# Folding w3 and w_out at the start, in two passes around the first attention, and the keys' sums inside the second product

## The chip, the cores and the metric

The kernel runs on one core of one Trainium2 chip, as one launch. The metric is the device time of an execution in microseconds (us). Before the change three runs gave a median of 1324.92 us (1324.34 to 1325.64).

## The reference

Three layers follow each other; all numbers are float32 except the weights of the second layer, which arrive as float64.

1. Attention with pooled keys: q, k and v are (8 batches, 8 heads, 576 positions, 64). Keys and values are averaged over groups of 8 positions, so each head has 72 keys. `attn = softmax(q @ k_p.T / 8)`, `out = attn @ v_p`; the heads are put side by side to `x`, 4608 rows of 512.
2. A gated layer without a nonlinearity: `a = x @ w1`, `b = x @ w2` (512 to 1024), `h = (a * b) @ w3` (1024 to 1024), `x2 = h @ w_out` (1024 to 512).
3. A mixture of 8 experts: `logits = x2 @ w_gate + bias`, the row's best expert is taken, `out = p * (relu(x2 @ w1[e]) @ w2[e])`.

Since nothing stands between w3 and w_out, `(a * b) @ w3 @ w_out` is `(a * b) @ W` with `W = w3 @ w_out` (1024 by 512). The kernel computes W once: this is the fold. It also computes `W @ w_gate` (the gate), whose 8 columns ride along with W, so that logits come out of the same matmuls as x2.

## The kernel before, in words

**Number format.** Every large matmul is made of three with operands split into a high and a low part (`mm3`, L116): high·high, high·low, low·high. Each matmul has 512 columns, or 260 in the second product. A float64 weight tile of 128 by 512 (0.52 MB) is turned into such a pair by `conv` (L390): two ScalarE steps on the two halves of each 8-byte number, two VectorE (DVE) steps that put the float32 together in place (L397, L399), a ScalarE copy to the high part (L400) and a subtraction on GpSimd (POOL) for the low part (L122). There are 40 such tiles: 16 of w3, 8 of w_out, 8 each of w1 and w2.

**Stages.** The 4608 rows go in 9 chunks of 512 (4 tiles of 128).

- Prologue: attention of chunk 0 (`Attention(0)`: K keys' sums, S scores and softmax, V1 values' sums, T transposes, V product), with w1 and w2 tiles 0 to 7 staged in the space of Wh and Wl (`stage`).
- `first_chunk` (L614): the first product of chunk 0 (`mm1`, L531; eight m blocks of 24 matmuls, `prep_w12(m + 2)` hooked behind block m) with scores of chunk 1 behind blocks 1, 3, 5 and 6; then `w_fold` (L433), which holds all eight PSUM banks as eight accumulators, converts w_out and w3 of round j = 0 to 7 and runs 24 matmuls a round; copies of W out of PSUM; `w_gate` (L465); the rest of attention 1; and the second product of chunk 0 (`mm_w`, L551; 4 tiles of 48 matmuls).
- Chunk loop: `next_chunk(ch)` (L635) for ch = 1 to 7 runs the first product of ch with attention ch + 1 hooked behind its blocks, S(0) to S(3) behind blocks 0 to 3, V1 behind 4, T behind 5 to 7, and the second product with V behind tiles 0 and 2 and early loads of `v` behind tile 3.
- Then routing's last part and the experts, which the change does not touch.

**What sets the order.** Inside the chunk loop the order of every engine is the order of the program text. Before it, a planner orders each engine's instructions by their place in the program and by when it expects them to be ready. DMAs are issued by SyncE (SP) in one queue, in order; a DMA that waits for a buffer holds those behind it.

**Lines that matter.** `S(i)` (L358) runs K for its tile, the scores (L270), loads `q` of the next tile (L361, one of two buffers), and K for the next tile. K leads to `prep_k(b)` (L176) when a new batch begins: four DVE sums (L183), two scalings into `kblk` (L188), and the load of the next batch's keys into the buffers just read (L173). The scores of an even tile use the one PSUM pair `sc`; in the chunk loop all tiles do. PSUM has four banks `mm`, two `tp` and the pair `sc`. Seven buffers of 4 KB per partition, `st4`, serve transposed tiles (`aT`, five an attention), early `v` and raw weight tiles.

Of the kernel before, what the change touches and what calls it, by code (L numbers as in the profile page):

```python
# [18 lines left out]
POOL = 8  # L19
# [8 lines left out]
T0 = (0, 1, 2, 3, 4)  # L28
ACT_T, MM_T = (0, 1, 2, 4, 5, 6, 7), (1, 2, 3)
CVN = 2  # L30
V_POOL, RAW = 2, 4
EARLY = 2
S1 = (1, 3, 5, 6)
# [59 lines left out]
def _program(outer, tc, nc, I, out):  # L93
# [68 lines left out]
    def load_k(b):  # L162
        if b == 0:
            kr = abp.tile([P, 4, S], F32, name="kr0", tag="abh")
# [38 lines left out]
    def load_v0():  # L203
        v0.append(abp.tile([P, 4, D, POOL], F32, name="vr0", tag="abl"))
# [7 lines left out]
    def early_v(b):  # L212

        if b < B:
# [41 lines left out]
    def softmax_tile(t):  # L256
        load_q(t)
        q = qs[t]
        if t in MM_T:
            sc = [(tp_ps if t == 3 else mm_ps)("scm") for _ in range(2)]  # L260
# [61 lines left out]
    def attn_V(a, z, aT, xh, xl):  # L322
        kn = slice(0, 6 * TK)
        for pr in range(4):
            ps = mm_ps("avps")[:, :z - a]
# [12 lines left out]
    class Attention:  # L338
# [19 lines left out]
        def S(self, i):  # L358
# [3 lines left out]
            if i < 3:  # L362
                self.K(i + 1)
# [10 lines left out]
        def V(self):  # L374
# [5 lines left out]
            attn_V(a, z, self.aT, *self.x)  # L380
# [27 lines left out]
    names = ("w1h", "w1l", "w2h", "w2l")  # L408
    w_stack = ExitStack()
    w12 = pool(w_stack, "w12")  # L410
    wt12 = [{n: w12.tile([P, 4, P], F32R, name=f"{n}{m}") for n in names} for m in range(8)]
    done_w = set()

    def prep_w12(m):
        if m < 8 and m not in done_w:
            done_w.add(m)
            conv(I["w1"][m], flat(wt12[m]["w1h"]), flat(wt12[m]["w1l"]), staged.get((m, "w1")))
            conv(I["w2"][m], flat(wt12[m]["w2h"]), flat(wt12[m]["w2l"]), staged.get((m, "w2")))


    staged = {}

    def stage(srcs):

        for n, tag in enumerate(("Wh", "Wl")):
            t = wp.tile([P, 4, 512], I64, name="stage", tag=tag)
            for i, (k, src) in enumerate(srcs[4 * n:4 * n + 4]):
                nc.sync.dma_start(t[:, i], src)
                staged[k] = t[:, i]

    fold = [((j, k), I["wo"][j] if k == "wo" else I["w3"][j, k]) for j in range(8) for k in ("wo", 0, 1)]

    def w_fold():  # L433
        sc = psum.tile([P, 2, 512], F32, name="wps3", tag="sc", bufs=1)
        accs = [sc[:, 0], sc[:, 1]] + [tp_ps("wps2") for _ in range(2)] + [mm_ps("wps") for _ in range(4)]
        for j in range(8):
            if j == 1:
                for k, src in fold[8:8 + CVN]:
                    staged[k] = load64(src)
                stage(fold[8 + CVN:16 + CVN])  # L440
            wo = st4("wo", (P, 2, 512), F32R)
            conv(I["wo"][j], wo[:, 0], wo[:, 1], staged.get((j, "wo")))
            if j == 0:
                w3 = [st4("w3", (P, 2, 4, P), F32R) for _ in range(2)]
            else:
                w3 = xp.tile([P, 2, 2, 4, P], F32R, name="w3", tag=("xh", "xl")[j % 2])
                w3 = [w3[:, 0], w3[:, 1]]
            for h in range(2):
                conv(I["w3"][j, h], flat(w3[h][:, 0]), flat(w3[h][:, 1]), staged.get((j, h)))
                for k in range(4):  # L450
                    mm3(accs[4 * h + k], w3[h][:, 0, k], w3[h][:, 1, k], wo[:, 0], wo[:, 1], j == 0, j == 7)
        Wh = wp.tile([P, 8, 2, 260], F32R, name="Wh", tag="Wh")
        Wl = wp.tile([P, 8, 2, 260], F32R, name="Wl", tag="Wl")

        wfs = []
        for kb in range(8):
            w2v = accs[kb].rearrange("p (h n) -> p h n", h=2)
            nc.scalar.copy(Wh[:, kb, :, :256], w2v)
            wf = st4("wf", (P, 2, 256), F32)
            (nc.scalar.copy if kb % 2 else nc.vector.tensor_copy)(wf, w2v)  # L460
            nc.vector.tensor_tensor(Wl[:, kb, :, :256], w2v, Wh[:, kb, :, :256].bitcast(F32), op=ALU.subtract)
            wfs.append(wf)
        return Wh, Wl, wfs

    def w_gate(Wh, Wl, wfs):  # L465

        gT = st4("gT", (E, 2, 512), F32)
        for half in range(2):
            wT = xp.tile([P, 4, 4, P], F32, name="wT", tag=("xh", "xl")[half])
            for k in range(4):  # L470
                tps = tp_ps("wtp", (P, 4, P))
                wf = wfs[4 * half + k]
                for nb in range(4):
                    nc.tensor.transpose(tps[:, nb], wf[:, nb // 2, P * (nb % 2):P * (nb % 2) + P], ident)
                (nc.scalar.copy if k % 2 else nc.vector.tensor_copy)(wT[:, :, k], tps)
            g = mm_ps("wgp")
            for nb in range(4):
                nc.tensor.matmul(g[:E], lhsT=wg[:, nb], rhs=flat(wT[:, nb]), start=nb == 0, stop=nb == 3)
            nc.scalar.copy(gT[:, half], g[:E])
        gp = tp_ps("wgt", (P, 8, 2, 4))  # L480
        for kb in range(8):
            nc.tensor.transpose(gp[:, kb].rearrange("p a b -> p (a b)"), gT[:, kb // 4, P * (kb % 4):P * (kb % 4) + P], ident[:E, :E])
        nc.scalar.copy(Wh[:, :, :, 256:260], gp)  # L483
        nc.vector.tensor_tensor(Wl[:, :, :, 256:260], gp, Wh[:, :, :, 256:260].bitcast(F32), op=ALU.subtract)

    att = Attention(0)
    att.K(0)
    for t in range(1, 4):
        load_q(t)
    nc.sync.dma_start(c, I["c"])  # L490
    load_v0()
    stage([((m, k), I[k][m]) for m in range(4) for k in ("w1", "w2")])
    for i in range(4):
        att.S(i)
        if i == 0:
# [432 lines left out]
```

## Time and profile before

| | |
|---|---|
| runs, median (lowest to highest) | 1324.92 us (1324.34 to 1325.64) |
| profiled execution, own time | 1322.37 us |
| its span | 1320.6 us, 17555 instructions |
| PE, matmuls | busy 1236.5 us (94%), 6518 instructions |
| DVE | busy 676.7 us (51%), 1325 |
| ScalarE (ACT) | busy 381.9 us (29%), 813 |
| POOL | busy 405.2 us (31%), 463 |
| TensorE's granted clock, mean | 0.970 of full speed |
| DMA | 126.99 MB, mean 96 GB/s |

The span runs from the first to the last instruction; the execution's own time is 1.8 us longer. Shares are means over stages that differ: DVE has 51% over the whole span and far more in some stretches, so each stage is read by itself. Matmuls are pipelined, so that a matmul's duration is longer than the distance between the starts of two; work is counted by that distance. A wait is read from the idle time in front of an instruction and from what ended it. A granted clock of 1.00 is 2.4 GHz, 0.50 is 1.2 GHz.

### The profile page before, as it was taken

The page shows a single profiled execution, that of the slowest core. Times are in us where ns is not written, and L with a number is a line of the kernel's source. Part 1 is how long each engine was busy: PE and PEld are TensorE (multiplying, and loading weights), DVE is VectorE, ACT ScalarE, POOL GpSimd, SP SyncE. Part 2 cuts the span into 40 slices and gives each one's busy share as a digit, 9 for nine tenths or more (in the row PEclk, how much of TensorE's full clock was granted, in tenths as well). Part 3 has the DMA queues.
Part 4 walks back from the last instruction along what each step waited for, and adds up shares of the span by engine and source line. Part 5 has one row for each costly group of instructions (what it writes and reads, how often), then busy time and mean ns, then how long its engine had stood idle before and what let it go on. Part 6 is the DMA issues. An engine that isn't in the chain of part 4 may idle for free. (4 is left out here: it accounts for less than half of the span.)

```text
span 1320.6 us, 17555 instructions
## 1 busy us (share of the span) xinstructions
PE 1236.5 (94%) x6518; PEld 1048.9 (79%) x6518; DVE 676.7 (51%) x1325; ACT 381.9 (29%) x813; POOL 405.2 (31%) x463
## 2 busy tenths in 40 slices
PE   4988798999989989999899999999999999999987
PEld 3766577897978979879789798887888888888877
DVE  6999525436344363343543523745464474556442
ACT  5786532322322223223222221211222212222211
POOL 3576301402314014050140301314543344244242
PEclk7989898999999999999999999998999999999998
DMA  8545212012021130210202001305441442344140
GB/s 291 211 167 202 91 49 80 9 65 79 17 77 52 47 97 9 93 44 25 84 1 87 14 25 50 127 24 184 176 170 46 176 176 95 121 175 168 53 170 18
DMA packets 53371, 126.99 MB, mean 96 GB/s; under 512 B 12668, under 2 KB 12924, under 8 KB 53244
## 3 DMA queue, kind: packets, MB, share of 16 engines
q1 hardware_dynamic: 45884, 105.89, 23.2%
q0 software_dynamic: 7232, 19.71, 3.8%
q8 instruction: 57, 0.93, 0.3%
q14 instruction: 54, 0.44, 0.1%
q10 hardware_dynamic: 144, 0.02, 0.0%
HBM read 105.62 MB, written 20.55 MB: 96 GB/s over the span
## 5 line engine op out<-in xcount | busy, mean ns | idle before, releaser
L299 POOL TENSOR_TENSOR ex<-ex,sm 128x576 f32<-128x576 f32 x35 | 40.5, 1157 | 442.8 <-DVE sm L293 423.7
L117 PE MATMUL e<-xh,e1h 128*128 128x512 f32 (+2 forms) x320 | 122.4, 383 | 5.7 <-issue 4.5
L118 PE MATMUL e<-xl,e1h 128*128 128x512 f32 (+2 forms) x320 | 123.0, 384 | 0.0
L117 PE MATMUL w<-xh,w1h 128*128 128x512 f32 x288 | 120.2, 417 | 1.9 <-ACT w1h L400 1.9
L119 PE MATMUL e<-xh,e1l 128*128 128x512 f32 (+2 forms) x320 | 121.4, 379 | 0.6 <-issue 0.6
L119 PE MATMUL e<-e2h,abl 128*128 128x512 f32 x296 | 117.8, 398 | 3.5 <-DVE abl L738 3.5
L117 PE MATMUL e<-e2h,abh 128*128 128x512 f32 x296 | 118.3, 400 | 1.3 <-DVE abl L738 1.3
L119 PE MATMUL w<-xh,w1l 128*128 128x512 f32 x288 | 115.7, 402 | 2.8 <-POOL w1l L122 2.8
L561 PE MATMUL x2ps<-Wh,abh 128*128 128x260 f32 x576 | 117.4, 285 | 0.3 <-ACT Wh L483 0.3
L561 PE MATMUL x2ps<-Wl,abh 128*128 128x260 f32 x576 | 116.6, 283 | 0.0
L118 PE MATMUL e<-e2l,abh 128*128 128x512 f32 x296 | 116.4, 393 | 0.0
L561 PE MATMUL x2ps<-Wh,abl 128*128 128x260 f32 x576 | 115.9, 283 | 0.0
L117 PE MATMUL w<-xh,w2h 128*128 128x512 f32 x288 | 113.3, 393 | 2.8 <-DVE asb L545 2.8
L118 PE MATMUL w<-xl,w1h 128*128 128x512 f32 x288 | 115.4, 401 | 0.0
L545 DVE TENSOR_TENSOR asb<-asb,w 128x512 f32<-128x512 f32 x72 | 49.4, 686 | 126.2 <-PE w L119 79.4
L119 PE MATMUL w<-xh,w2l 128*128 128x512 f32 x288 | 113.3, 393 | 0.0
L118 PE MATMUL w<-xl,w2h 128*128 128x512 f32 x288 | 112.8, 392 | 0.0
L546 ACT CAST abh<-asb 128x512 fp32r<-128x512 f32 x72 | 44.6, 620 | 192.3 <-DVE asb L545 192.3
L737 ACT ACTIVATE abh<-e 128x512 fp32r<-128x512 f32 (+2 forms) x80 | 45.4, 567 | 169.8 <-PE e L119 157.2
L750 POOL DMA_INDIRECT out<-o,idc x37 | 37.5, 1012 | 182.7 <-ACT o L749 161.9
L566 DVE TENSOR_TENSOR lg<-x2ps,bias 128x4 f32<-128x4 f32 x72 | 11.6, 162 | 155.9 <-ACT x L565 151.9
L561 PEld LDWEIGHTS x2ps<-Wh,abh 128*128 128x128 f32 x576 | 89.3, 188 | 0.7 <-ACT Wh L483 0.4
(203 smaller groups left out, 2650.6 us busy)
## 6 DMA issues: line engine op xcount, KB each, us to landing
raw<-ew_in SPq DMA_DIRECT2D x80, 512.0 KB
stage<-w_in SPq DMA_DIRECT2D x19, 512.0 KB
kr<-k_in SPq DMA_DIRECT2D x32, 288.0 KB
q<-q_in SPq DMA_DIRECT2D x36, 256.0 KB
vr<-v_in SPq DMA_DIRECT2D x36, 256.0 KB
x2d<-x SPq DMA_DIRECT2D x36, 256.0 KB
cv<-w_in SPq DMA_DIRECT2D x13, 512.0 KB
vr<-v_in SPq DMA_DIRECT2D x54, 64.0 KB
```

Source lines behind the costliest of these rows:

```text
L117: nc.tensor.matmul(ps, lhsT=wh, rhs=xh, start=start, stop=False)
L118: nc.tensor.matmul(ps, lhsT=wh, rhs=xl, start=False, stop=False)
L119: nc.tensor.matmul(ps, lhsT=wl, rhs=xh, start=False, stop=stop)
L299: eng.tensor_tensor(e3, e3, bc(sm.unsqueeze(2), [P, H, SP_]), op=ALU.mult)
L545: nc.vector.tensor_tensor(a, a, ps[1], op=ALU.mult)
L546: nc.scalar.copy(abh[:, m], a)
L561: nc.tensor.matmul(pss[hf][:, :260], lhsT=l[:, m, cols], rhs=r[:, m, hf], start=m == 0 and r is Wh and l is abh, stop=m == 7 and l is abl)
L566: nc.vector.tensor_tensor(lg[:, i, 4 * hf:4 * hf + 4], pss[hf][:, 256:260], bias[:, t, 4 * hf:4 * hf + 4], op=ALU.add)
L737: nc.scalar.activation(hT[0][:, m, :w], ps[:, :w], AF.Relu)
L750: nc.gpsimd.indirect_dma_start(out=out, out_offset=bass.IndirectOffsetOnAxis(idc[:, i, 0:1], 0), in_=o, in_offset=None, bounds_check=N - 1 ...
```

## The change

- The fold comes first, in two passes. Pass one (`accs`, the four `mm` banks) takes the w_out tiles and the first half of w3; rounds 0 to 3 of it follow S(0) to S(3) of attention 0, round 4 V1, rounds 5 and 6 T. Then V. Pass two (`accs2`: `sc` and the two `tp` banks) takes the second half of w3. The converted w3 and w_out tiles lie in the space that w1 and w2 get afterwards; raw tiles go through a ring of eleven buffers (Wh, Wl and free parts of the two 16 KB buffers of k and v), each loaded when the one eleven places before has been converted.
- `conv` writes its intermediate values to a contiguous scratch buffer (`scr`, one of `st4`) in place of the strided halves of the raw tile.
- W's copies out of PSUM follow pass two and the conversion of w1 and w2 tile 0; gate and the rest of attention 1 are hooked into the first product of chunk 0; the values of batch 1 are loaded early there.
- `S(i)` loads `q` two tiles ahead. In the chunk loop the keys' sums and the load of the next keys no longer follow S; they are hooked behind tile 1 of the second product of the chunk before.
- The first attention's V uses the `tp` banks; tile 2's scores use `sc`, tile 1's `tp`.

The diff, cut to its core:

```diff
-ACT_T, MM_T = (0, 1, 2, 4, 5, 6, 7), (1, 2, 3)
+ACT_T, MM_T = (0, 1, 2, 4, 5, 6, 7), (1, 3)
...
-        if b < B:
+        if b < B and b not in v_raw:
             pairs = [st4("vr2", (P, 2, D, POOL), F32) for _ in range(3)]
...
             load_q(4 * self.ch + i + 1)
-            if i < 3:
+            load_q(4 * self.ch + i + 2)
+            if i < 3 and self.ch < 2:
                 self.K(i + 1)
...
-            attn_V(a, z, self.aT, *self.x)
+            attn_V(a, z, self.aT, *self.x, tp_ps if self.ch == 0 else mm_ps)
...
+    def conv(raw, hi, lo):
+        s = st4("scr", (P, 2, 512), I32)
+        f, m, t = s[:, 0].bitcast(F32), s[:, 0], s[:, 1]
+        nc.scalar.activation(f, raw.bitcast(F32)[:, 1::2], AF.Copy, scale=float(2.0 ** -112))
+
+        nc.scalar.activation(t, raw.bitcast(U32)[:, 0::2], AF.Copy, scale=TOP_S, bias=TOP_B)
+        nc.vector.scalar_tensor_tensor(out=t, in0=m, scalar=3, in1=t, op0=ALU.logical_shift_left, op1=ALU.bitwise_or)
+        nc.vector.scalar_tensor_tensor(out=m, in0=m, scalar=-2147483648, in1=t, op0=ALU.bitwise_and, op1=ALU.bitwise_or)
         nc.scalar.copy(hi, f)
         sub_pool(lo, f, hi)
...
+    ring = [x[:, i] for x in [wp.tile([P, 4, 512], I64, name="stage", tag=tag) for tag in ("Wh", "Wl")] for i in range(4)]
+    ring += [ab0["abl"][:, 1024:1536], ab0["abl"][:, 1536:2048], ab0["abh"][:, 1152:1664]]
...
+    wf = [w12.tile([P, 2, 2, 512], F32R, name=f"f{m}", tag=w_tag(m), bufs=1) for m in range(8)]
+    w3s = [wf[j // 2][:, j % 2] for j in range(8)]
+    wos = [wf[4 + j // 2][:, j % 2] for j in range(8)]
+    order = [x for j in range(8) for x in (("wo", j), ("w3", j, 0))] + [("w3", j, 1) for j in range(8)]
...
+    def fold_conv(k):
+        dst = wos[k[1]] if k[0] == "wo" else w3s[k[1]]
+        conv(raws[k], dst[:, 0], dst[:, 1])
+        fold_load()
+
+    def fold_mm(accs, j):
+        w3, wo = w3s[j].rearrange("p t (k n) -> p t k n", k=4), wos[j]
+        for k in range(4):
+            mm3(accs[k], w3[:, 0, k], w3[:, 1, k], wo[:, 0], wo[:, 1], j == 0, j == 7)
...
+    accs = [mm_ps("wps") for _ in range(4)]
+    for j in range(8):
+        if j < 4:
+            att.S(j)
+        if j == 4:
+            att.V1()
+        if j == 5:
+            sct = psum.tile([P, 2, 512], F32, name="sct", tag="sc", bufs=1)
+            att.T((0, 1), {0: sct[:, 0], 1: sct[:, 1]})
+            att.T((2, 3))
+        if j == 6:
+            sct = psum.tile([P, 2, 512], F32, name="sct", tag="sc", bufs=1)
+            att.T((4,), {4: sct[:, 0], 5: sct[:, 1]})
+        for k in order[2 * j:2 * j + 2]:
+            fold_conv(k)
+        fold_mm(accs, j)
+    att.V()
...
+    accs2 = [sc[:, 0], sc[:, 1]] + [tp_ps("wps2") for _ in range(2)]
+    for j in range(8):
+        fold_conv(order[16 + j])
+        fold_mm(accs2, j)
     prep_w12(0)
...
+    wfs = [fold_out(accs, 0)]
+    wfs.append(fold_out(accs2, 1))
+    W = (Wh, Wl)
+    prep_w12(1)
...
         h1 = {m: [lambda m=m: prep_w12(m + 2)] for m in range(8)}
-        for n, m in enumerate(S1):
-            h1[m].append(lambda n=n: att.S(n))
-        h1[0] += [lambda: att.K(0)]
-        h1[3] += [lambda: stage(fold[:8])]
+        h1[0] += [lambda: att.K(0), lambda: w_gate_out(w_gate(wfs[0]), 0)]
+        h1[1] += [lambda: w_gate_out(w_gate(wfs[1]), 1)]
+        for i in range(4):
+            h1[i + 1] += [lambda i=i: att.S(i)]
+        h1[4] += [lambda: early_v(1)]
+        h1[6] += [att.V1, lambda: att.T((0, 1))]
+        h1[7] += [lambda: load_k(2), lambda: att.T((2, 3)), lambda: att.T((4,))]
         ab = mm1(0, x_first, h1)
-        W = w_fold()
-        w_gate(*W)
...
-        mm_w(0, ab, lgs[0], {0: [att.V], 2: [att.V], 3: [lambda: early_v(2)]}, W)
+        mm_w(0, ab, lgs[0], {0: [att.V], 1: [lambda: need(prep_k, 2)], 2: [att.V], 3: [lambda: early_v(2)]}, W)
...
-        mm_w(ch, ab, lgs[ch % 2], {0: [att.V], 2: [att.V], 3: [lambda: early_v(b)]}, W)
+        mm_w(ch, ab, lgs[ch % 2], {0: [att.V], 1: [lambda: need(prep_k, b)], 2: [att.V], 3: [lambda: early_v(b)]}, W)
```

`fold_out` copies four accumulators out of PSUM with the three instructions that `w_fold` had for each (L458, L460, L461); `w_gate` now takes one half of W, with two half-size copies where one whole copy stood (L475), and `w_gate_out` writes the gate's columns of that half.

## Rows read from the trace of the kernel before

**Rows 1.** Busy time by stage: length, PE, PEld, DVE, ACT, POOL, clock, DMA share, GB/s.

```profile
0.00:36.00 36.00, 19.18 (x70) 15.12 (x71) 22.67 (x52) 19.24 (x70) 12.71 (x28) 0.76 0.88 294
36.00:133.00 97.00, 85.94 (x363) 67.46 (x362) 93.06 (x116) 76.00 (x179) 61.61 (x46) 0.95 0.53 191
133.00:175.00 42.00, 34.17 (x131) 19.99 (x130) 19.39 (x29) 20.54 (x37) 10.49 (x7) 0.88 0.22 76
211.25:797.95 586.70, 558.05 (x3313) 494.73 (x3313) 257.68 (x604) 152.27 (x320) 131.06 (x220) 0.98 0.16 50
797.95:1320.60 522.65, 503.06 (x2382) 417.57 (x2381) 273.03 (x492) 104.01 (x182) 189.29 (x164) 0.98 0.33 121
```

**Rows 2.** Timeline around the prologue's end: start, duration, instruction, idle before it.

```profile
147.28 0.69 DVE L399 SCALAR_TENSOR_TENSOR cv<-cv 128x512 int32<-128x512 int32 x1
...
174.94 0.51 PE L561 MATMUL x2ps<-Wh,abh 128*128 128x260 f32 x2 [0.30 <-ACT Wh L483]
```

**Rows 3.** PE's waits, 178 to 760 us: waiter, releaser, sum, times, longest.

```profile
PE sc L270 <- DMA q<-q_in: 18.7, 6, 4.4
PE sc L270 <- issue: 8.4, 3, 4.3
PE sc L270 <- DVE kblk L188: 1.3, 1, 1.3
```

**Rows 4.** Timeline of PE, second scores of two chunks.

```profile
222.24 2.26 PE L270 MATMUL sc<-kblk,q 128*128 128x144 f32 x8 [4.28 <-issue]
...
305.50 3.76 PE L270 MATMUL sc<-kblk,q 128*64 128x144 f32 x16 [2.62 <-DMA q<-q_in]
```

**Rows 5.** Timeline of DVE ahead of 222.24 us.

```profile
216.18 0.76 DVE L289 TENSOR_TENSOR ex<-sc,mx 128x576 f32<-128x576 f32 x1
...
218.80 2.68 DVE L183 TENSOR_REDUCE ks<-kr 128x72 f32<-128x576 f32 x4
221.51 0.62 DVE L188 TENSOR_SCALAR kblk<-ks 64x288 f32<-64x288 f32 x2
```

**Rows 6.** Timeline of SP's queue ahead of 305.50 us.

```profile
293.78 3.95 SPq L199 DMA_DIRECT2D vr<-v_in  x6
297.77 0.42 SPq L254 DMA_DIRECT2D q<-q_in  x1
```

**Rows 7.** Timeline of PE in the fold, at either clock.

```profile
103.15 0.39 PE L119 MATMUL wps<-wo,w 128*128 128x512 f32 x1
103.38 0.39 PE L117 MATMUL wps<-wo,w 128*128 128x512 f32 x1
...
125.80 0.63 PE L118 MATMUL wps<-wo,w 128*128 128x512 f32 x1
126.22 0.63 PE L119 MATMUL wps<-wo,w 128*128 128x512 f32 x1
```

**Rows 8.** Busy time in one second product (columns as in Rows 1).

```profile
269.00:292.00 23.00, 23.00 (x181) 22.77 (x181) 6.52 (x22) 6.76 (x20) 0.00 (x0) 1.00 0.09 35
```

**Rows 9.** Busy time behind two of the waits (columns as in Rows 1).

```profile
222.00:230.00 8.00, 7.76 (x28) 6.68 (x29) 4.16 (x8) 1.89 (x3) 1.62 (x3) 0.68 0.53 166
...
646.00:650.00 4.00, 4.00 (x18) 3.30 (x17) 2.65 (x5) 1.15 (x2) 0.00 (x0) 0.87 0.23 70
```

**Rows 10.** Timeline of DVE, then POOL, in the fold.

```profile
122.16 0.68 DVE L397 SCALAR_TENSOR_TENSOR stage<-stage 128x512 int32<-128x512 int32 x1
...
126.45 1.80 DVE L399 SCALAR_TENSOR_TENSOR stage<-stage 128x512 int32<-128x512 int32 x1
...
126.40 1.30 POOL L122 TENSOR_TENSOR wo<-stage,wo 128x512 fp32r<-128x512 f32 x1
```

**Rows 11.** Groups by line, 0 to 178 us: busy, mean ns, idle before.

```profile
L399 DVE SCALAR_TENSOR_TENSOR stage<-stage 128x512 int32<-128x512 int32 x24 | 24.8, 1045 | 0.3
L397 DVE SCALAR_TENSOR_TENSOR stage<-stage 128x512 int32<-128x512 int32 x24 | 22.5, 944 | 1.5 <-ACT stage L396 1.4
...
L299 POOL TENSOR_TENSOR ex<-ex,sm 128x576 f32<-128x576 f32 x7 | 8.4, 1198 | 10.7 <-DVE sm L293 6.1 <-ACT vbt L246 3.9 <-ACT wo L400 0.7
```

More of the change, by code (lines that the diff above doesn't have):

```diff
@@ L163, in load_k @@
         if b == 0:
-            kr = abp.tile([P, 4, S], F32, name="kr0", tag="abh")
+            kr = ab0["abh"].bitcast(F32)[:, :4 * S].rearrange("p (a s) -> p a s", a=4)
             for pr in range(4):
@@ L203, in load_v0 @@
     def load_v0():
-        v0.append(abp.tile([P, 4, D, POOL], F32, name="vr0", tag="abl"))
+        v0.append(ab0["abl"].bitcast(F32)[:, :2048].rearrange("p (a d w) -> p a d w", a=4, d=D))
         v0.append([at.tile([P, D, POOL], F32, name="vr", tag="raw", bufs=RAW) for _ in range(2)])
@@ L259, in softmax_tile @@
         if t in MM_T:
-            sc = [(tp_ps if t == 3 else mm_ps)("scm") for _ in range(2)]
+            sc = [tp_ps("scm") for _ in range(2)]
         else:
@@ L405, in run @@
             f()
-    names = ("w1h", "w1l", "w2h", "w2l")
     w_stack = ExitStack()
     w12 = pool(w_stack, "w12")
-    wt12 = [{n: w12.tile([P, 4, P], F32R, name=f"{n}{m}") for n in names} for m in range(8)]
-    done_w = set()
-    def prep_w12(m):
[L415 to L418, printed above, removed]
@@ L421, in _program @@
[L421 to L463, printed above, removed]
@@ L465, in w_gate @@
[L465 to L484, printed above, removed]
+    ab0 = {n: abp.tile([P, 2048], I64, name=f"early{n}", tag=n) for n in ("abh", "abl")}
@@ new lines, in fold_out, with w_gate @@
+    def fold_out(accs, h):
+        wf = w12.tile([P, 4, 2, 256], F32, name="wf", tag=w_tag(4 + h), bufs=1)
+        for k in range(4):
+            kb = 4 * h + k
+            w2v = accs[k].rearrange("p (h n) -> p h n", h=2)
+            nc.scalar.copy(Wh[:, kb, :, :256], w2v)
+            (nc.scalar.copy if k % 2 else nc.vector.tensor_copy)(wf[:, k], w2v)
+            nc.vector.tensor_tensor(Wl[:, kb, :, :256], w2v, Wh[:, kb, :, :256].bitcast(F32), op=ALU.subtract)
+        return wf
+    def w_gate(wf):
+        wT = [st4("wT", (P, 2, 4, P), F32) for _ in range(2)]
+        for k in range(4):
+            tps = tp_ps("wtp", (P, 4, P))
+            for nb in range(4):
+                nc.tensor.transpose(tps[:, nb], wf[:, k, nb // 2, P * (nb % 2):P * (nb % 2) + P], ident)
+            for n in range(2):
+                (nc.scalar.copy if k % 2 else nc.vector.tensor_copy)(wT[n][:, :, k], tps[:, 2 * n:2 * n + 2])
+        g = tp_ps("wgp")
+        for nb in range(4):
+            nc.tensor.matmul(g[:E], lhsT=wg[:, nb], rhs=flat(wT[nb // 2][:, nb % 2]), start=nb == 0, stop=nb == 3)
+        gT = st2("gT", (E, 512))
+        nc.scalar.copy(gT, g[:E])
+        return gT
@@ new lines, in w_gate_out, with load_w12 @@
+    def w_gate_out(gT, h):
+        gp = tp_ps("wgt", (P, 4, 2, 4))
+        for k in range(4):
+            nc.tensor.transpose(gp[:, k].rearrange("p a b -> p (a b)"), gT[:, P * k:P * k + P], ident[:E, :E])
+        kb = slice(4 * h, 4 * h + 4)
+        nc.scalar.copy(Wh[:, kb, :, 256:260], gp)
+        nc.vector.tensor_tensor(Wl[:, kb, :, 256:260], gp, Wh[:, kb, :, 256:260].bitcast(F32), op=ALU.subtract)
+    names = ("w1h", "w1l", "w2h", "w2l")
+    wt12 = []
+    raw12 = {}
+    def load_w12(m):
+        if m < 8 and m not in raw12:
+            raw12[m] = [load64(I[n][m], st4("cv", (P, 512), I64)) for n in ("w1", "w2")]
@@ L486, in _program @@
+    def prep_w12(m):
+        if m < 8 and m == len(wt12):
+            load_w12(m)
+            t = w12.tile([P, 4, 4, P], F32R, name=f"w{m}", tag=w_tag(m), bufs=1)
+            wt12.append({n: t[:, i] for i, n in enumerate(names)})
+            for i in range(2):
+                conv(raw12[m][i], flat(t[:, 2 * i]), flat(t[:, 2 * i + 1]))
     att = Attention(0)
+    fold_load()
+    fold_load()
     att.K(0)
+    nc.sync.dma_start(c, I["c"])
+    for _ in range(2):
+        fold_load()
     for t in range(1, 4):
@@ L489, in _program @@
         load_q(t)
-    nc.sync.dma_start(c, I["c"])
+    for _ in range(3):
+        fold_load()
     load_v0()
[L492 to L495, printed above, removed]
-            need(prep_v1, 0)
-    att.V1()
-    att.T(T0, [tp_ps("atp") for _ in range(2)] + [mm_ps("atp") for _ in range(4)])
-    prep_w12(0)
-    att.V()
-    for m in range(1, EARLY):
-        prep_w12(m)
-    nc.scalar.dma_start(wg, I["wg"])
+    for _ in range(4):
+        fold_load()
```

49 lines of the change are left out of this document (19 added, 30 removed).

## The prediction

> **What bounds the kernel now.** The page's first part gives TensorE (PE) 94% of the span: at most 84 us are idle, plus what a lower clock costs. I then cut the span into stages [rows 1]. The last one, from 797.95 us on, holds nothing that the diff touches; its 522.65 us stay. Two parts remain.
>
> The prologue ends where the second product of chunk 0 starts, at 174.94 us [rows 2]. VectorE (DVE) is what to read there: busy 22.67 of the first 36 us, 93.06 of the next 97, 19.39 of the last 42 [rows 1]. So it is the bound in the middle (96%) and has 39.9 us free at the two ends: at the start little but the first attention is given to it, and after the last `conv` (147.28 us [rows 2]) fold copies and gate run as a chain between PE, ScalarE and DVE.
>
> In the chunk loop, 211.25 to 797.95 us, that is seven chunks of 83.8 us, DVE is busy 257.68 of 586.70 us and PE 558.05 [rows 1]: PE is the bound, and its losses are in the list of its waits. Three rows hold nearly all: the score matmuls wait 18.7 us for `q` in six places, 8.4 us for "issue" in three, 1.3 us for `kblk` [rows 3], together 28.4 us. The second kind is keys' sums too: PE stands 4.28 us until 222.24 [rows 4], while DVE runs the sums from 218.80 and the scaling to 222.13 [rows 5].
>
> **The change part by part.**
>
> *Chunk loop: q.* The load of `q` is issued at 297.77, behind the `v` tail loads from 293.78 on the same queue (SP) [rows 6], and PE gets it at 305.50 after 2.62 us [rows 4]. The change loads two tiles ahead. The load issued after a chunk's first scores is then for the third tile: it lands at about 305.4 again, and is wanted one m block after 302.9, where PE now arrives at the second scores (305.50 − 2.62). A block is 24 matmuls at 0.227 (103.15 to 103.38 us [rows 7]) and about 1.1 us of scores, 6.6 us, so it is wanted at 309.5: 4 us to spare. A `q` buffer is free once the scores of two tiles before are done; SP waits there for these matmuls, and behind it stand only loads wanted later. All 18.7 us go.
>
> *Chunk loop: keys' sums.* The 2.68 + 0.62 us of DVE work [rows 5] move from between the blocks of the first product to behind tile 1 of the second. There PE is busy 23.00 of 23 us and DVE 6.52 [rows 8], so 3.3 us lie beside matmuls; behind them on DVE wait the logits of tile 2, due a tile (a quarter of the 23 us) later. The load of the next keys, which waits for these sums on SP, moves with them; x2d stores and early `v` loads stand behind it, none wanted within the stage. If that cover went, the cost would be the same 3.3 us a chunk. The 8.4 + 1.3 us go. What is late next is the score bank: DVE frees it at 216.94 [rows 5] and PE would come at 217.96 (222.24 − 4.28), so nothing.
>
> *Chunk loop: clock.* After the longer waits the granted clock is at 1.2 GHz for a while: mean 0.68 over 222 to 230 us, 0.87 over 646 to 650, first and last of six such stretches [rows 9]. Twice (1 − clock) times the length gives the time at the lower level, 18 us over the six, of which half, 9 us, is lost. It goes with the waits. Loop: 28.4 + 9 = 37 us. Bounds: if only the keys' waits go, 9.7 us and a third of the clock's, 13 us; all, 38.
>
> *Prologue: DVE's budget.* The kinds of work do not change: 40 `conv`s (24 for w3 and w_out, 16 for w1 and w2), two attentions, fold copies, gate. DVE was busy 22.67 + 93.06 + 19.39 = 135.1 us before the second product [rows 1]. Added: the last five subtractions behind the second attention's transposes, which now run after 175 us, 5 × 0.68; eight more copies in the gate, of half size, half of them on DVE at about 0.4 (an estimate from 0.68 for the whole size): 5 us, so 140. A private scratch in place of work on the strided halves I count as nothing; a strided DVE step alone takes 0.68 us [rows 10], as long as DVE's other steps of 512, which bounds the gain by a few hundredths of a microsecond a step and the loss likewise. What DVE cannot fill: the first raw tiles (two of 0.52 MB at 294 GB/s [rows 1], and a first latency) arrive at about 5 us, and the last block of the first product, 24 × 0.227 = 5.4 us, follows the last conversion. Between, the saturated stretch idles 4%; I take 8%, 11 us, since in the first pass transfers gate too: the first keys stand behind two raw tiles (3.6 us), and 24 raw tiles with the attention's 4 MB need 56 us of the queue. Sum 5 + 140 + 11 + 5 = 161 us, against 175: a gain of 14. Bounds: no bubbles, 150 (gain 25); all 39.9 us of idle kept and the 5 us added, 180 (loss 5).
>
> *Prologue: PE as a check.* The fold's 192 matmuls (43.6 us) no longer stand behind the first product; half of them lie beside the first attention. Until that product begins, 26 `conv`s pass DVE at 1.99 us each (1.045 + 0.944 [rows 11]), 52 us, with the first attention's 23, the 5 us at the start and 8%: 86 us. All eight PSUM banks are held by the two passes' sums until the fold copies have run, some 4 us more. PE was busy 139.3 us before 175 [rows 1]; without the fold's 43.6 and the first 36 us' 19.2 it then owes at most 76, less at full clock: 155 to 166. 161 stands.
>
> *A rule weighed.* A DVE step of `conv` takes 0.68 us alone and 1.80 where GpSimd's (POOL's) subtraction of 1.30 us began just before it [rows 10]. The Trainium skill, "SBUF — State Buffer", section "Who interferes with whom", says why: a DVE instruction with two SBUF inputs and a GpSimd instruction share a port pair, and whoever issues first holds it for the whole instruction. The trace agrees (1.80 against 0.68). This speaks against packing conversions densely, and is a rival below.
>
> **The sum.** 14 + 37 = 51 us off the profiled execution's 1322.37 gives 1271. That execution lies 2.5 us under the runs' median (1324.92), so I predict 1273 us; own range 1260 to 1285.
>
> **The rivals.**
>
> *DVE and POOL exclude each other, and this sets the prologue.* A `conv` needs 2 × 0.6 on DVE and 1.30 on POOL, one after the other: 2.5 us, 100 for forty. With POOL's 8.4 us of normalising [rows 11], DVE's 55 us of other work (135 − 40 × 1.99) beside none of it and 10 at the ends, 173: no gain. For it: mean steps of 0.944 and 1.045 against 0.68 [rows 10, 11]. Against: if DVE's other work reads PSUM or sums one operand, it can lie beside POOL. Loop alone: 1322.4 − 37 + 2.5 = 1288.
>
> *Low clock in the passes.* In pass one PE has 12 matmuls per two conversions, 2.7 us in some 5. In the first 36 us, with many gaps, the clock was 0.76 in the mean; in the saturated stretch, where the fold also waited between bursts, 0.95 [rows 1]. At 0.43 us a matmul (125.80 to 126.22 [rows 7]) the passes cost 82 us in place of 44; with attention at the same level the first product starts about 18 us later: 1273 + 18 = 1291. The Trainium skill, "TensorE: Matmul & The Clock Gate", section "HAM oscillation — how this bites in real kernels", describes bursts between waits that run cold every time; the 0.95 agrees only in part.
>
> *q still late.* If the loads land late whatever the distance, the loop gives 13: 1322.4 − 14 − 13 + 2.5 = 1298. Against it: the 4 us to spare.
>
> *DVE fully packed.* 150 us in place of 161: 1262.
>
> *Slower: scratch buffers starve the conversions.* Each `conv` now also needs one of the seven buffers called st4, which five transposed tiles, three early `v` pairs, the raw w1 and w2 tiles and the gate's transposes share. With one left, a `conv` is a chain: three ScalarE steps (some 2 us by DVE's 0.68 for the same size), DVE 1.99, POOL 1.30, so 5.3 us, against 3.8 in the forecast (151 us over 40). At 1.5 each the 51 us are used up when 34 of 40 go so; with all, 1333. Against: five tiles are held only from round 5 of pass one to the end of the first attention, which leaves two, and the `v` pairs come when two loads are left.
>
> **How the numbers follow.** Forecast 0.52, exclusion 0.17, low clock 0.08, q late 0.09, fully packed 0.08, slower 0.06. The range 1250 to 1303 holds the first five: under 1260 since DVE's stretched steps may stretch less, above 1298 for two cases together. A difference under 0.2% (2.6 us) can't be told from none here; only a few of the starving cases end there: 0.02. Slower 0.06, faster 0.92.
>
> **What would show it.** In the changed profile: no PE wait of over 1 us for `q` or keys' sums in the loop, chunks of about 78.5 us at a clock of 1.00, the sums inside the second product's stretch; the second product of chunk 0 starting at about 161 us, DVE over 85% busy from 6 us on. Wrong if that start is at 175 or later, if the score matmuls wait for something new (the bank, PSUM), or if `conv`s come more than 4 us apart while DVE idles.

## The result, and the profile after

The changed kernel takes 1278.1 us (median; 1274.7 to 1281.2) beside 1324.6 us of the kernel before on the same chip: ratio 0.9649, 95% interval 0.9617 to 0.9681, 46 us less. The forecast was 1273, its range 1250 to 1303. The total agrees, its two terms do not: the loop gave 42 us where 37 were forecast; the prologue, where 14 were, gave 3 (up to the start of chunk 1 in the profiled executions) to 5 (put in alone, `e3` below).

Busy time by stage of the profiled execution (1275.6 us, span 1273.8), columns as in [rows 1]; the fourth row is the same work as there, from the start of chunk 1 to the end of the seventh loop chunk:

```profile
0.00:36.00 36.00, 18.70 (x63) 13.39 (x64) 24.50 (x45) 21.00 (x70) 18.35 (x29) 0.92 0.92 323
36.00:133.00 97.00, 82.16 (x334) 56.76 (x333) 80.64 (x115) 67.16 (x138) 46.78 (x34) 0.93 0.49 164
133.00:175.00 42.00, 38.10 (x181) 31.31 (x181) 28.15 (x46) 26.83 (x85) 16.21 (x17) 0.96 0.36 118
208.31:753.38 545.07, 544.90 (x3315) 486.24 (x3314) 256.58 (x598) 151.38 (x320) 132.46 (x220) 1.00 0.16 49
753.38:1273.80 520.42, 501.08 (x2382) 416.09 (x2381) 271.50 (x492) 103.99 (x182) 189.15 (x164) 0.99 0.33 122
```

The loop fell from 586.70 to 545.07 us, 41.6 less, 77.9 a chunk. PE is now busy 544.90 of 545.07: nothing is left there but its own matmuls. The last stage, which the diff does not touch, is 2.2 us shorter. PE's waits from 130 to 760 us (waiter, releaser, sum, times, longest) answer to [rows 3]; the prologue's last 44 us are in the window too:

```profile
PE w L113 <- ACT w L394: 1.7, 1, 1.7
PE sc L266 <- ACT ex L281: 1.2, 1, 1.2
PE w L115 <- POOL w L118: 1.1, 1, 1.1
PE rps L624 <- DVE r_oh L617: 0.2, 1, 0.2
```

The waits for `q`, "issue" and `kblk` are gone; the first three of these four lie in the prologue. The keys' sums now run inside the second product, on DVE between the logits of two tiles, as this stretch of DVE's timeline shows (start, duration, instruction, idle before it; it answers to [rows 5, 8]):

```profile
503.09 0.43 DVE L592 TENSOR_TENSOR lg<-x2ps,bias 128x4 f32<-128x4 f32 x2 [3.64 <-ACT x L591]
503.44 2.72 DVE L179 TENSOR_REDUCE ks<-kr 128x72 f32<-128x576 f32 x4
506.20 0.62 DVE L184 TENSOR_SCALAR kblk<-ks 64x288 f32<-64x288 f32 x2
508.90 0.44 DVE L592 TENSOR_TENSOR lg<-x2ps,bias 128x4 f32<-128x4 f32 x2 [2.08 <-ACT x L591]
```

DVE is idle again after them for 2.08 us until the next tile's logits: the cover holds.

The prologue's end answers to [rows 2]. The view lists the operations of one tile name: duration (ns, least/median/most), first to last start. The first row is the first product of chunk 0, the second the second products:

```profile
L113 PE MATMUL w<-xh,w x64: 387/389/628, 98.3 to 172.6; 128*128 128x512 f32 x64
...
L587 PE MATMUL x2ps<-Wh,abh x576: 278/282/393, 174.1 to 821.8; 128*128 128x260 f32 x192
```

The second product begins at 174.1 us in place of 174.94; 161 was forecast. Until 174.1 DVE is busy 132.4 us (24.50 + 80.64 + 28.15, less the last 0.9 us), against 135.1 before: so it idles 42 us where the forecast left it 21. Its conversion steps up to the first product are as long as they were in [rows 11] (line groups, 0 to 98 us: busy, mean ns, idle before):

```profile
L393 DVE SCALAR_TENSOR_TENSOR scr<-scr 128x512 int32<-128x512 int32 x26 | 26.7, 1033 | 0.5
L392 DVE SCALAR_TENSOR_TENSOR scr<-scr 128x512 int32<-128x512 int32 x27 | 24.9, 926 | 1.1 <-ACT scr L391 1.0
```

### The profile page after: what moved, and what is told of

The parts are those of the page before. It is cut to its first block, busy times and chain, and to the rows that moved or that the text cites. A ratio compares the mean times of both kernels' runs of the same rounds, so it can differ in the third digit from the quotient of the medians.

```text
span 1273.8 us, 17569 instructions
## 1 busy us (share of the span) xinstructions
PE 1218.2 (96%) x6518; PEld 1035.8 (81%) x6518; DVE 672.2 (53%) x1329; ACT 379.7 (30%) x818; POOL 403.0 (32%) x463
## 5 line engine op out<-in xcount | busy, mean ns | idle before, releaser
L113 PE MATMUL w<-xh,w 128*128 128x512 f32 x576 | 230.2, 400 | 4.0 <-DVE asb L571 2.3
L115 PE MATMUL w<-xh,w 128*128 128x512 f32 x576 | 226.5, 393 | 1.1 <-POOL w L118 1.1
L114 PE MATMUL w<-xl,w 128*128 128x512 f32 x576 | 225.2, 391 | 0.0
L113 PEld LDWEIGHTS w<-xh,w 128*128 128x128 f32 x576 | 108.8, 189 | 26.8 <-DVE asb L571 2.7
L115 PEld LDWEIGHTS w<-xh,w 128*128 128x128 f32 x576 | 108.8, 189 | 24.7 <-POOL w L118 1.5
L114 PEld LDWEIGHTS w<-xl,w 128*128 128x128 f32 x576 | 108.7, 189 | 21.8 <-issue 0.9
L769 POOL DMA_INDIRECT out<-o,idc x37 | 37.5, 1014 | 183.3 <-ACT o L768 168.8
L587 PEld LDWEIGHTS x2ps<-Wl,abh 128*128 128x128 f32 x576 | 88.9, 188 | 0.0
```

Source lines behind the costliest of these rows:

```text
L113: nc.tensor.matmul(ps, lhsT=wh, rhs=xh, start=start, stop=False)
L114: nc.tensor.matmul(ps, lhsT=wh, rhs=xl, start=False, stop=False)
L115: nc.tensor.matmul(ps, lhsT=wl, rhs=xh, start=False, stop=stop)
L587: nc.tensor.matmul(pss[hf][:, :260], lhsT=l[:, m, cols], rhs=r[:, m, hf], start=m == 0 and r is Wh and l is abh, stop=m == 7 and l is abl)
L769: nc.gpsimd.indirect_dma_start(out=out, out_offset=bass.IndirectOffsetOnAxis(idc[:, i, 0:1], 0), in_=o, in_offset=None, bounds_check=N - 1 ...
```

## Experiments

Chips differ by a few microseconds, so ratios to the kernel before on the same chip are compared; 0.001 is 1.3 us.

**The two halves alone.** Each half of the change was put in without the other.

`e3_prologue_alone` is the changed kernel with both loop edits taken back (and the hook behind tile 1 removed):

```diff
-            load_q(4 * self.ch + i + 2)
-            if i < 3 and self.ch < 2:
+            if i < 3:
```

> The changed kernel with both edits of the loop undone: only the new prologue is left. Theory (the loop is the gain): 1278 and 42 us, about 1320 us, 2 to 5 us under the kernel before. Rival (the prologue gives the 14 us that were forecast, part of it hidden in the loop): about 1310 us.

Measured: 1314.9 us, 0.9959 (0.9938 to 0.9981). The prologue alone is worth 5 us (2.5 to 8): the theory's 2 to 5, not the rival's 10 and more.

`e4_loop_alone` is the kernel before with these edits alone:

> The kernel before with the two edits of the loop alone (q two ahead, keys' sums behind tile 1 of the second product); the fold stays behind the first product. Theory (the loop is the gain): about 1282 us. Rival (loop and prologue need each other, since the early values of batch 1 free the buffers for the keys): over 1295 us.

Measured: 1276.8 us, 0.9688 (0.9657 to 0.9719): 41 us, and no difference from the changed kernel that the intervals can tell. PE's waits from 205 to 760 us have one row left, and the second product starts at 175.8:

```profile
PE rps L599 <- DVE r_oh L592: 0.2, 1, 0.2
...
L562 PE MATMUL x2ps<-Wh,abh x576: 278/282/393, 175.8 to 825.1; 128*128 128x260 f32 x192
```

41 + 5 = 46: the halves add up, and the loop is nearly all of it.

**The loop's two edits, each taken back alone.** `e1_q_one_ahead` drops the second load:

```diff
             load_q(4 * self.ch + i + 1)
-            load_q(4 * self.ch + i + 2)
```

> The changed kernel with q loaded one tile ahead again; all else as changed. Theory (distance): the load behind a chunk's first scores still stands behind ten loads of v, so the second scores of each chunk wait 2.4 to 4.4 us again, about 19 us of waits and some 8 us at the lower clock: about 1304 us. Rival (keys' load in the way): q was late since the next keys' load, which waits for the sums, stood in front of it on the queue; with the sums moved, one tile ahead is enough: about 1279 us.

Measured: 1298.7 us, 0.9843 (0.9822 to 0.9864). PE's waits from 205 to 760 us:

```profile
PE sc L266 <- DMA q<-q_in: 14.1, 5, 4.0
```

So distance is what the second load brings; a `q` one tile ahead is late again. The clock goes with it: for the loop's matmuls PE is busy 553.90 us (208 to 776 us, mean clock 0.98), 9 more than the 544.90 at 1.00 in the changed kernel.

`e2_keys_behind_scores` lets the keys' sums follow the scores as before:

```diff
-            if i < 3 and self.ch < 2:
+            if i < 3:
                 self.K(i + 1)
...
-        mm_w(ch, ab, lgs[ch % 2], {0: [att.V], 1: [lambda: need(prep_k, b)], 2: [att.V], 3: [lambda: early_v(b)]}, W)
+        mm_w(ch, ab, lgs[ch % 2], {0: [att.V], 2: [att.V], 3: [lambda: early_v(b)]}, W)
```

> The changed kernel with the keys' sums behind the scores in the first product again; q stays two ahead. Theory: the waits for keys' sums return, 9.7 us and some 5 us at the lower clock: about 1293 us, with PE waiting in front of the scores only in chunks in which a new batch begins. Rival: with q in time PE comes earlier to the scores and waits longer for the same sums, 3.3 us in each of seven chunks and more clock: about 1305 us.

Measured: 1308.6 us, 0.9922 (0.9892 to 0.9952), the rival's result. The same view:

```profile
PE sc L266 <- issue: 10.4, 3, 4.3
PE sc L266 <- DVE kblk L184: 6.8, 3, 3.1
```

The sums' waits are 17.2 us here; beside late loads they were 9.7 [rows 3]. PE no longer waits for `q`, comes sooner to the same sums, and waits there instead. From the prologue alone (0.9959) the `q` load alone brings 0.0037 (5 us, which the two intervals can hardly tell from nothing), the keys alone 0.0116 (15 us; the lower bound of the prediction was 13 for this case), both 0.031 (41 us).

**What holds the prologue.** `a1_changed_again` repeats the changed kernel beside the next ones:

> The changed kernel itself, on the same chip as the others: 1275 to 1281 us, the second product of chunk 0 at about 174 us.

Measured: 1277.5 us, 0.967 (0.9639 to 0.9701), second product from 175.0. Over the five profiled executions with this prologue (the changed kernel twice, e1, e2 and e3, whose edits are aimed at the loop) that start lies between 173.6 and 176.5 us, so a difference of some 3 us between two single executions tells nothing.

`p1_low_parts_zero` takes the subtraction from POOL: the low parts of all 40 converted tiles are filled with zeros there:

```diff
-        sub_pool(lo, f, hi)
+        nc.gpsimd.memset(lo.bitcast(F32), 0.0)
```

> The changed kernel with the low parts of all 40 converted weight tiles set to zero by a POOL fill in place of the subtraction; everything else runs as before on the same tiles. POOL then reads nothing for a conversion. Exclusion theory (DVE and POOL in turn set the prologue): DVE's two steps fall to 0.68 us each, both passes are through by about 80 us instead of 98, and the second product of chunk 0 starts at about 158 or sooner instead of 174. PE theory (from the end of the passes on, PE's own 68 us of matmuls set the pace): the passes end some 10 us sooner, and the first product still takes about 72 us.

Measured: 1263.4 us in one execution, span 1261.5. Tiles, and DVE's groups from 0 to 174 us:

```profile
L113 PE MATMUL w<-xh,w x64: 389/389/632, 91.7 to 158.8; 128*128 128x512 f32 x64
...
L587 PE MATMUL x2ps<-Wh,abh x576: 277/282/393, 160.2 to 807.8; 128*128 128x260 f32 x192
...
L392 DVE SCALAR_TENSOR_TENSOR scr<-scr 128x512 int32<-128x512 int32 x40 | 28.6, 718 | 7.9 <-ACT scr L391 7.7
L393 DVE SCALAR_TENSOR_TENSOR scr<-scr 128x512 int32<-128x512 int32 x40 | 27.5, 693 | 0.8
```

Both steps are back at 0.7 us, the first product starts 6.6 us sooner, the second 14. What POOL does in the conversions costs this prologue 14 us. Of the exclusion theory's numbers the second product's start came out nearly (158 or sooner), the others of both theories did not: the passes end at 91.7 us, not about 80, and the first product takes 68.5 us, less than the PE theory's 72.

`p4_fold_high_only` asks for PE's share: two of the fold's three products are left out (64 matmuls in place of 192):

```diff
-            mm3(accs[k], w3[:, 0, k], w3[:, 1, k], wo[:, 0], wo[:, 1], j == 0, j == 7)
+            nc.tensor.matmul(accs[k], lhsT=w3[:, 0, k], rhs=wo[:, 0], start=j == 0, stop=j == 7)
```

> The changed kernel with only the product of the high parts in the fold: 64 matmuls in place of 192, W less exact; all conversions stay. Both engines are full from 78 to 98 us in the changed kernel, so this tells which of them counts there. PE theory: pass two loses 14.5 us of its 21.8 us of matmuls, the first product begins before 90 us instead of at 98, and the second product of chunk 0 starts at 162 to 166. DVE theory (conversions in turn with POOL): the first product cannot begin before its own tiles are converted and W's copies are made, 95 us or later, and the second product starts at 171 or later.

Measured: 1271.0 us in one execution; first product from 92.7, second from 172.2. PE's waits up to 176 us, and busy time by stretch:

```profile
PE wps L430 <- ACT f L394: 19.1, 11, 7.2
...
PE w L113 <- ACT w L394: 9.9, 2, 7.7
...
60.00:98.00 38.00, 24.93 (x59) 16.49 (x60) 35.19 (x43) 29.31 (x54) 20.07 (x14) 0.67 0.43 138
```

With 128 matmuls less (29 us at 0.227 [rows 7]) the passes end only 5.6 us sooner, between the two theories (before 90, or 95 and later): PE now waits 19 us for converted tiles. Conversions set the pace of the passes more than the fold's matmuls do. The second product starts 1.9 us sooner than the changed kernel's 174.1, less than the spread of those five; PE waits 9.9 us before converted w1 and w2 tiles, 7.7 of them inside the first product.

`p2_no_gate` leaves the gate out (its 8 columns are zeros, so routing and the whole time are not comparable):

```diff
-        h1[0] += [lambda: att.K(0), lambda: w_gate_out(w_gate(wfs[0]), 0)]
-        h1[1] += [lambda: w_gate_out(w_gate(wfs[1]), 1)]
+        h1[0] += [lambda: att.K(0), lambda: no_gate(0)]
+        h1[1] += [lambda: no_gate(1)]
```

> The changed kernel without the gate's transposes, copies and matmuls in the first product; the gate's eight columns are zero, so that all rows go to the expert that the bias prefers and the time of the experts' part is another: only the prologue is read. PE theory: the first product of chunk 0, now 76 us (98 to 174), shortens by the gate's 12 us of PE work and its two waits of 2.3 and 2.5 us, to about 60. DVE theory (conversions and attention on DVE set it): by the gate's eight DVE copies of 0.4 us, 3 us, to about 72.

Measured: first product from 97.8, second from 162.0:

```profile
L592 PE MATMUL x2ps<-Wh,abh x576: 277/282/393, 162.0 to 810.1; 128*128 128x260 f32 x192
```

So 64.2 us between them, against 75.8 (the PE theory had 60, the DVE theory 72): the gate's work, 12 us of PE, lies on the path inside the first product.

**Versions.** `c1_early_v_later` moves the early loads of `v` one block later, so that they take their st4 buffers after the last raw w1 and w2 tiles:

```diff
-        h1[4] += [lambda: early_v(1)]
+        h1[5] += [lambda: early_v(1)]
```

> The changed kernel with the early loads of batch 1's values hooked behind block 5 of the first product instead of block 4, behind the last conversion. Theory (the three buffers that these values take hold up the last two raw weight tiles, loaded only at 153 us): the 1.7 and 1.1 us that PE waits at 165 and 167 us go, with 2 us of lower clock: second product of chunk 0 at about 170 instead of 174, 1274 us if the changed kernel has 1278. Rival: the values' sums then come late, and the transposes behind them: 174 or later.

Measured: 1269.7 us, 0.9612 (0.958 to 0.9645), second product from 169.0. SP's queue in the changed kernel, then in this one:

```profile
144.05 3.07 SPq L191 DMA_DIRECT2D vr<-v_in  x4
147.22 2.71 SPq L195 DMA_DIRECT2D vr<-v_in  x4
...
153.28 0.83 SPq L383 DMA_DIRECT2D cv<-w_in  x2
```

```profile
143.69 1.81 SPq L383 DMA_DIRECT2D cv<-w_in  x2
...
151.55 2.62 SPq L191 DMA_DIRECT2D vr<-v_in  x4
```

The last two raw tiles are issued 9.6 us sooner, and the waits of 1.7 and 1.1 us for their conversion (the waits above) are gone. It gains 5 us by ratio against the first runs of the changed kernel, where the intervals overlap, and 8 against the repeated ones on the same chip, where the runs do not (1268.3 to 1271.8 and 1274.9 to 1278.6).

`c2_low_parts_on_vector` adds to this that DVE does all subtractions itself:

```diff
-        sub_pool(lo, f, hi)
+        nc.vector.tensor_tensor(lo, f, hi.bitcast(F32), op=ALU.subtract)
```

> The kernel with the later early values (1269.7 us) with the subtractions of all 40 conversions on DVE instead of POOL. Exclusion theory: a conversion then takes 3 x 0.6 = 1.8 us of the pair instead of 2.5, and DVE's stretched steps fall to 0.68: the second product of chunk 0 starts some 5 us earlier than 169, about 1264 us. Rival (DVE's own time counts, 1.96 us a conversion now, 1.9 to 2.0 with three steps): no change, 1270, or slower where DVE has other work.

Measured: 1259.9 us, 0.9544 (0.9521 to 0.9567), second product from 155.4. DVE's groups, 0 to 174 us:

```profile
L392 DVE SCALAR_TENSOR_TENSOR scr<-scr 128x512 int32<-128x512 int32 x40 | 27.9, 715 | 2.4 <-ACT scr L391 2.3
L393 DVE SCALAR_TENSOR_TENSOR scr<-scr 128x512 int32<-128x512 int32 x40 | 27.0, 692 | 0.1
L395 DVE TENSOR_TENSOR f<-scr,f 128x512 fp32r<-128x512 f32 x24 | 16.2, 692 | 0.4
```

From c1's 169.0 that is 13.6 us sooner, nearly three times the 5 us of the exclusion theory: POOL's subtractions cost much here, but not at that theory's price.

`c3_half_on_vector` gives DVE every second one:

```diff
+        nconv.append(1)
+        if len(nconv) % 2:
+            sub_pool(lo, f, hi)
+        else:
+            nc.vector.tensor_tensor(lo, f, hi.bitcast(F32), op=ALU.subtract)
-        sub_pool(lo, f, hi)
```

> As the last, but only every second conversion subtracts on DVE. Exclusion theory: 2.15 us of the pair per conversion, half the gain, about 1267 us. Rival (a balance of both engines is best, since POOL works beside DVE's steps that read PSUM): better than all on one, about 1264.

Measured: 1257.4 us, 0.953 (0.9508 to 0.9552), the lowest median of all, though not to be told from c2; first product from 89.6, second from 154.7. Tile, and busy time by stretch:

```profile
L593 PE MATMUL x2ps<-Wh,abh x576: 278/282/385, 154.7 to 803.2; 128*128 128x260 f32 x192
...
60.00:98.00 38.00, 37.25 (x164) 29.64 (x164) 37.81 (x57) 32.01 (x59) 13.80 (x8) 1.00 0.30 100
98.00:174.00 76.00, 73.92 (x421) 58.22 (x421) 53.65 (x104) 45.28 (x139) 15.96 (x17) 1.00 0.47 161
```

Half of the subtractions moved gives all of the gain; the exclusion theory's half of it (1267 us) is refuted, and the rival's balance, better than all on one, is not shown either.

`e5_old_prologue_half` asks whether folding first is worth anything then: the old prologue, with the loop's edits and the subtractions split as in c3.

> The kernel before with the two edits of the loop, and every second subtraction of a conversion on VectorE: the prologue's order is the old one. It tells whether folding first is worth something once VectorE and POOL no longer hold each other. Order theory (the new order lets VectorE be filled, the old one leaves it idle at both ends however fast its steps are): in the old prologue VectorE was full only from 36 to 133 us; there its conversions shorten by some 0.9 us each (1.99 to about 1.6 for two steps, plus half a subtraction of 0.69), so about 26 conversions times 0.05 to 0.4 us, 1 to 10 us: second product from about 166 to 174 us (175.8 without it), time about 1270 (1266 to 1276), 9 to 16 us behind the changed kernel's prologue with the same edit (1257.4, start 154.7). Rival, exclusion theory alone (the order is worth nothing, the whole gain is the subtractions'): start at about 157 to 160 us, time about 1260.

Measured: 1272.8 us, 0.9635 (0.9591 to 0.968); second product from 170.6, where the old order had it at 175.8 without the split. Busy time by stage:

```profile
0.00:36.00 36.00, 18.84 (x72) 14.68 (x73) 22.91 (x52) 19.37 (x70) 12.70 (x28) 0.76 0.89 293
36.00:133.00 97.00, 87.78 (x378) 67.72 (x376) 94.01 (x139) 77.49 (x183) 38.37 (x30) 0.98 0.56 198
133.00:175.00 42.00, 35.36 (x148) 22.12 (x149) 21.21 (x34) 19.97 (x36) 3.31 (x2) 0.84 0.26 101
```

The old order idles on DVE at both ends as before (13 us of the first 36, 21 of the last 42). The order theory's numbers came out. The new order starts its second product at 154.7, 16 us sooner, 14 in the time by the ratios (0.9635 − 0.953). But c3 also has c1's later `v` loads: with these and all subtractions on POOL the order is worth 6.8 us there (175.8 − 169.0), without them 1.7 (175.8 − 174.1). So 9 of the 16 us come only with half of POOL's subtractions moved; the same split gave the old order 5.2 (175.8 − 170.6).

## Why the prediction was right, and where it was not

**Chunk loop: q.** Right: no wait is left, and taken back (e1) it is 14.1 us of waits again.

**Chunk loop: keys' sums.** Right: the sums lie beside matmuls, with 2.08 us of DVE idle behind them.

**Chunk loop: clock.** The mechanism was right, the term too small: 9 us forecast, 13.2 measured, the fall of PE's busy time for the same matmuls (558.05 to 544.90; the clock is now 1.00). I had added up six stretches and taken 18 us at the lower level; read in stretches of 2 us over the whole loop of the trace before, it was 24, so 12 lost. What the text didn't see is that the two waits hide each other: their rows (18.7 and 9.7) are what each costs beside the other, and e2's 17.2 shows one alone. For the sum this did no harm, since both went.

**Prologue: DVE's budget.** This is the step that failed: DVE was to be full from the first tiles to the last block of the first product, "Between, the saturated stretch idles 4%; I take 8%, 11 us", and with it 5 + 140 + 11 + 5 = 161. DVE's busy time came out below the 140 (132), but its idle time was 42 where the sum had 21. The stretched steps were in the sum: 26 conversions were put at 52 us up to the first product and took 51.6 (26.7 + 24.9). What the text did not draw from its rows is what such a step is: 0.94 or 1.04 us [rows 11] is 0.7 of work, and the rest is waiting for POOL's subtraction, booked as busy. DVE's timeline of the changed kernel in pass two, and POOL's under it, answer to [rows 10]:

```profile
72.04 0.68 DVE L392 SCALAR_TENSOR_TENSOR scr<-scr 128x512 int32<-128x512 int32 x1
72.76 0.69 DVE L393 SCALAR_TENSOR_TENSOR scr<-scr 128x512 int32<-128x512 int32 x1
73.45 1.71 DVE L392 SCALAR_TENSOR_TENSOR scr<-scr 128x512 int32<-128x512 int32 x1
75.19 1.80 DVE L393 SCALAR_TENSOR_TENSOR scr<-scr 128x512 int32<-128x512 int32 x1
...
72.86 1.75 POOL L118 TENSOR_TENSOR f<-scr,f 128x512 fp32r<-128x512 f32 x1 [2.01 <-ACT f L394]
75.16 1.29 POOL L118 TENSOR_TENSOR f<-scr,f 128x512 fp32r<-128x512 f32 x1 [0.55 <-ACT f L394]
```

POOL begins at 72.86 behind a running DVE step and takes 1.75; the next DVE step, at 73.45, takes 1.71; POOL begins at 75.16 and the DVE step of 75.19 takes 1.80. Each engine is stretched by the other, in turn. The Trainium skill, "SBUF — State Buffer", section "Who interferes with whom", says that whoever issues first holds the shared port pair for the whole instruction; the rows agree. This was the rival of 0.17, "this sets the prologue", and the start came where it put it (173), with "no gain". p1, c2 and c3 show by their second products (160 beside 174; 155 and 155 beside c1's 169) that POOL's subtractions cost some 14 us. That this is about what the forecast missed is chance, as DVE's times up to the second product show (p1, c1, c2, c3; columns as in [rows 1]):

```profile
0.00:160.20 160.20, 131.01 (x567) 100.40 (x568) 112.25 (x203) 112.01 (x290) 41.80 (x79) 0.94 0.60 203
0.00:169.00 169.00, 134.79 (x569) 98.43 (x569) 134.79 (x203) 114.11 (x290) 82.45 (x79) 0.94 0.57 191
0.00:155.40 155.40, 129.28 (x568) 98.87 (x569) 131.61 (x241) 112.33 (x290) 25.23 (x39) 0.97 0.60 209
0.00:154.70 154.70, 130.75 (x568) 97.37 (x569) 131.77 (x220) 113.32 (x290) 55.76 (x59) 0.96 0.60 209
```

p1 reaches 160 with DVE busy 112 us and idle 48, not with 140 and 21. And from c1 to c2 and c3 DVE's busy time hardly falls (134.8 to 131.6 and 131.8); its idle time does, from 34 us to 24 and 23.

Where the idle time of the changed kernel lies splits the miss in two. Up to the first product, at 98.3 us where the forecast had 90, DVE idles 17.8 us (5 and 8% made some 11), all but 0.4 of it before 60 us, and its other work takes 28.9 (the forecast had 23, and 4 for the fold copies). From 60 to 98 us it is full, 37.63 of 38 us with 43 instructions (c3: 37.81 with 57):

```profile
36.00:60.00 24.00, 16.24 (x63) 10.72 (x61) 18.11 (x25) 14.97 (x29) 13.09 (x10) 0.91 0.56 203
60.00:98.00 38.00, 35.72 (x139) 27.70 (x140) 37.63 (x43) 30.48 (x55) 23.24 (x15) 0.91 0.51 160
98.00:174.00 76.00, 67.30 (x305) 48.64 (x305) 52.05 (x92) 47.54 (x139) 26.66 (x26) 0.96 0.40 130
```

From there to the second product it takes 75.8 us (forecast 71), and here DVE is idle for 24 us: PE holds this stretch, not the engine that the budget was made for. It has 67 us of work at a clock of 0.96, 12 of it the gate's (p2: 11.6 us less without them), and stands still for most of 9 us, in front of the gate's transposes (4.8) and of conversions that come late (2.8). One reason for those is c1's: early `v` loads take the st4 buffers that the last raw tiles need. That is the mechanism of the rival on the slower side, in a small form: 5 to 8 us, not 51.

The scratch buffer's steps, counted as nothing, came out so where a step runs alone (0.68 and 0.69 us above, 0.68 [rows 10]). Over all 40 conversions the two steps took 72.0 us (37.3 + 34.7, up to 174.1 us) where they took 77.8 before; most of what DVE's busy time fell short of the 140 is this, and whether it comes from the scratch or from fewer meetings with POOL was not told apart.

Two readings in the prediction are off without moving the sum: the 39.9 us that it puts "at the two ends" is DVE's idle time over all three stretches (the ends have 35.9), and the 1.99 us a conversion is the mean of the 24 tiles in [rows 11]; over all 40 it was 1.95 (77.8 / 40).

**Prologue: PE as a check.** Its 155 to 166 is a bound on PE's work, and c2 and c3 reach it (155) once tiles come in time: from 90 us to its second product c2 has PE busy 65.40 of 65.40 us. As a confirmation of 161 it was worth little, since it held only if tiles came in time; but for the first product it looked at the right engine.

**The other rivals.** q was not late, and DVE was not packed: 42 us idle. Low clock in the passes was not decisive: 0.91 and 0.96 in the rows of the two stretches above. Where PE does stand and wait in turn, in p4, the mean is 0.67. The Trainium skill, "TensorE: Matmul & The Clock Gate", section "HAM oscillation — how this bites in real kernels", describes bursts between waits that start at the lower clock every time; p4's row agrees in part, since 0.67 lies between the two levels.

So the total was right in part by luck: an underestimated loop (+5) stood against an overestimated prologue (−13, with 0.8 in place of 14), and chunk 0's second product and the last stage gave some 4 us that were not forecast: the span fell by 0.8 (up to the second product), 2.1 (to chunk 1), 41.6 and 2.2 us, 46.8 in all, where 51 were forecast.

**Open.** p1, c2 and c3 take from POOL both what excludes DVE and the longer step (1.52 us in the mean of the forty, (38.1 + 22.5) / 40 by POOL's rows below, by 0.69 on DVE) in each conversion's chain. From 60 us to the first product, where DVE is full, the two steps of 14 conversions take 29.7 us of DVE in c1 and 18.4 in c2 (groups by line), where 9.4 of subtractions come back: 1.9 us less in all, while the first product starts 5.7 sooner; 3.0 of the rest are keys' sums, which c2 has elsewhere. How much of the first product's 10.7 us (75.8 to 65.1 in c3, of which c1 has 4.7) is the shorter chain, how much the exclusion, was not told apart. Nor were c1's gain and the clock: the prologue's time at the lower clock was 23.9 us in one profiled execution of the changed kernel, 37.5 in the other, and 20.3 in c1's (stretches of 4 us, twice 1 − clock times the length).

## What to carry to other kernels

Before an engine's busy time enters a budget, compare the mean duration of its instruction with the shortest of the same shape: what lies above is waiting for another engine, it does not go away by packing, and a reordering gains little until the cause is gone (here 2 us, 7 with the early loads moved, 16 with half of POOL's subtractions moved too). And make the budget stage by stage: DVE's was carried on into a stretch that PE held. Waits of one instruction for two causes are not a sum: each row tells what that cause costs beside the other, so forecast the removal of both together, and of one alone at what the other will then take. And a term that the trace bounds from 13 to 38 should be tested apart from one bounded from −5 to 25, since a right total can hide both being wrong.

## What the runs showed of the hardware

POOL's subtraction of a 128 by 512 tile takes 1.30 us where it begins first [rows 10] and more in the mean (changed kernel, groups of POOL's line up to 174 us: busy, mean ns, idle before), the same on DVE 0.69 (c2):

```profile
L118 POOL TENSOR_TENSOR f<-scr,f 128x512 fp32r<-128x512 f32 x24 | 38.1, 1600 | 34.1 <-ACT f L394 31.5 <-issue 1.3 <-PE wps L115 1.3
L118 POOL TENSOR_TENSOR w<-scr,w 128x512 fp32r<-128x512 f32 x16 | 22.5, 1416 | 32.6 <-ACT w L394 22.9 <-issue 9.7
```

Nearly the same time came from all forty on DVE (c2, 1259.9) and from twenty (c3, 1257.4), although the steps are 0.69 to 0.72 us long in the one and 0.78 to 0.82 in the other: the first pays in DVE's own subtractions what the second pays in waiting (81.9 and 79.1 us of DVE for conversions up to 174 us). That half and half would do no worse than none on POOL I had not expected from steps that are stretched to 1.80 us.
